# A broadcast read as 32 rows four times in place of 8 rows sixteen times, with a newly searched instruction order, in a two-layer linear-attention block

## Chip, cores and metric

The kernel runs on one core of one Trainium2 chip. The metric is the device time of one execution in microseconds (us), taken as the median of several executions. The program is straight-line code: 1618 operations before the change, put on the engines by a stored order that a search has found. One execution of each kernel was also recorded by the hardware profiler; all lines in profile fences below come from such records. "Span" is the time from the first to the last instruction in a record. It is about 1.7 us shorter than the device time of the same run.

## The reference, cut

```python
def _A_ref(x, wqkv, wo):                     # linear attention, 32 heads of 16
    q, k, v = split(x @ wqkv)                # (cut: reshape to heads)
    phi = lambda t: jnp.where(t > 0, t + 1, jnp.exp(t)) + 1e-6
    pq, pk = phi(q), phi(k)
    kv  = jnp.einsum("bhsd,bhse->bhde", pk, v)
    z   = jnp.einsum("bhsd->bhd", pk)
    num = jnp.einsum("bhqd,bhde->bhqe", pq, kv)
    den = jnp.einsum("bhqd,bhd->bhq", pq, z)[..., None] + 1e-6
    return merge_heads(num / den) @ wo
def _B_ref(x, w1, w2):                       # MLP, 512 -> 1376 -> 512
    return jnp.maximum(x @ w1, 0) @ w2
x = x + _A_ref(_layernorm(x), A_wqkv, A_wo)  # x: 1 x 2048 x 512, bfloat16
x = x + _B_ref(_layernorm(x), B_w1, B_w2)
x = x + _A_ref(_layernorm(x), A_wqkv, A_wo)
x = x + _B_ref(_layernorm(x), B_w1, B_w2)
```

The change concerns `den`. For each token and head there is one denominator, and all 16 elements of that head are divided by it. In the kernel the elements of eight heads lie on 128 partitions and 512 tokens lie along the free axis, so one row of reciprocals has to reach 16 partitions.

## The kernel before

The 2048 tokens are worked on in four chunks of 512, in each of the two attention layers, so the code below runs eight times. A small matmul against `Zc` writes the denominators of eight heads into 32 rows, each head four times. ScalarE forms the reciprocal as exp(-ln). Then the rows go out to DRAM and come back with every row repeated over 16 partitions, one DMA for each group of eight heads (`j`), and VectorE multiplies.

```python
def a_den_inv(t, b):
    us = [pq_unit(j, t) for j in range(4)]
    mm_group(lambda: [(psv[32*j:32*j+32, b, :], Zc[:, j, :], unit_ap(us[j]), True, True, False)
                      for j in range(4)], ...)
    ...                                                     # ACT: ln, then exp(-ln) -> rsp
    r = rdram[cur_layer[0] // 2, t]
    dma(lambda e: e.dma_start(r, rsp[:, s, :]), ...)        # L844, write
    for j in range(4):                                      # L847, broadcast
        i = 4 * t + j
        dma(lambda e, i=i, j=j: e.dma_start(xn[:, i, :],
            r[32*j:32*j+8, :].unsqueeze(1).broadcast_to([8, 16, 512])), [("rd", t)], [("xn", i)], 650.0, ...)

def a_den_mul(t, s, GB):                                    # L855, multiply
    for j in range(4):
        g.add(DVE, lambda e, j=j, i=i: e.tensor_tensor(unit_ap(us[j]), unit_ap(us[j]), xn[:, i, :], ALU.mult), ...)
```

Which head a row holds is decided by a mask made once on GpSimd. With the pattern `[[0, 4], [-16, 8]]` the eight heads come one after the other, and that four times over:

```python
e.affine_select(zm1[:],   onesf[:, 0:32], [[0, 4], [-16, 8]], ALU.is_ge, 0.0, base=0,  channel_multiplier=1)
e.affine_select(zmask[:], zm1[:],         [[0, 4], [16, 8]],  ALU.is_ge, 0.0, base=15, channel_multiplier=-1)
```

DMA transposes, issued on the same queue as the broadcasts, turn the normalised activations `xn` into `Tb`, which matmuls read:

```python
def tr_dma(lo, hi):                                         # L484
    dma(lambda e: e.dma_start_transpose(Tb[:, lo:hi, :, :]..., xn[:, lo:hi, :]...), ...)
```

Ten matmuls on zeros open the program on TensorE (`WARM`):

```python
for k in range(WARM):                                       # WARM = 10, on a tile of zeros
    last = e.matmul(psv[:, wt, :], wrm[:, 0:128], wrm[:, :], start=True, stop=True)
```

Two small constants, `ehead` and `esel`, are computed on VectorE by `den_consts()`; `esel` is made from `ehead`, and nothing reads `esel`. The order in which all operations are issued, and the memory bank of each matmul result, are two stored tables, `ORDER` and `BANKS`.

## Time and profile before

| | before |
|---|---|
| device time, 3 runs | 268.33, 268.69 and 552.36 us (median 268.69; the last counts as a slow run and is left out of every ratio) |
| span of the profiled run | 267.4 us (another run, of 269.12 us) |
| TensorE busy | 260.0 us, 97% |
| TensorE idle in the profiled run | 7.4 us: 2.0 in the first 10 us, 2.9 in the last 3.4 us, 2.5 between |
| broadcasts | 32 of 128 KB each, on 8 of 16 DMA engines |

How to read it: an engine that is 97% busy can be made faster only by the 7.4 us in which it stands, by gaps too short to show, or by less work. The change takes no work from TensorE. Two answers about single lines of the kernel before: count, then nanoseconds that the queue spends on issuing one (minimum, median, maximum), then the first and last start.

```profile
L844 SPq DMA_DIRECT2D rdram<-rsp x8: 322/334/572, 42.4 to 191.3; - x8
...
L847 SPq DMA_DIRECT2D xn<-rdram x32: 577/577/751, 44.2 to 197.6; - x32
```

The write and the broadcast move 128 KB each, but the broadcast takes the queue 577 ns and the write 334.

Last, the only wait of TensorE on a DMA, in the list of waits:

```profile
PE ps L538 <- DMA Tb<-xn: 1.0, 1, 1.0
```

It is one wait of 1.0 us, on a transpose.

### The profile page before, as it was taken

To read this page: it belongs to the slowest core of one execution; us is meant where nothing else is said; L and a number is where in the kernel's file an instruction comes from. 1 tells how busy PE (TensorE), PEld (TensorE's weight loads), DVE (VectorE), ACT (ScalarE), POOL (GpSimd) and SP (SyncE) were. 2 spreads that over 40 slices of the span, in tenths; PEclk is the share of its full clock that TensorE was granted. 3 is DMA by queue.
4 is the path that set the end of the run, shared out by engine and by line. 5 is a ranking of instruction groups with operands and counts; after the bars stand their busy time and mean duration, and the time that the engine had idled before them with its cause. 6 is when DMAs were issued, how large, how long until landed. Compare 5 with 4: busy or idle time off the path is not lost.

```text
span 267.4 us, 5269 instructions
## 1 busy us (share of the span) xinstructions
PE 260.0 (97%) x1919; PEld 171.5 (64%) x1937; DVE 240.7 (90%) x660; ACT 202.4 (76%) x446; POOL 19.6 (7%) x30
## 2 busy tenths in 40 slices
PE   7999999998999999999999999999999999999995
PEld 2444444546447888887875654454786778888883
DVE  4999999999789999999998998499989999889975
ACT  3999965889888786487788998799999869745320
POOL 4021000000030002201011000000000000130000
PEclk9999999999999999999999999999999999999999
DMA  6954882346234061401403400322592245201104
GB/s 209 382 115 82 195 306 71 127 78 162 38 107 91 0 81 21 82 0 22 77 13 69 78 2 2 103 93 43 131 175 50 39 42 99 81 0 22 80 2 157
DMA packets 47626, 23.61 MB, mean 88 GB/s; under 512 B 37008, under 2 KB 46192, under 8 KB 47600
## 3 DMA queue, kind: packets, MB, share of 16 engines
q1 hardware_dynamic: 47456, 23.24, 35.3%
q8 instruction: 15, 0.25, 0.4%
q14 instruction: 11, 0.09, 0.1%
q10 hardware_dynamic: 144, 0.03, 0.1%
HBM read 11.21 MB, written 3.15 MB: 54 GB/s over the span
## 4 chain that ended last, share of the span: by engine, by line
PE 85%; DVE 7%; DMA 5%; issue 1%; ACT 1%; SPq 0%; DVEq 0%
PE ps L538 84%; DMA Tb<-xn 3%; DMA xin<-in_A_x_dram 1%; DVE xres L551 1%; DVE xres L582 1%; DVE ps L1035 1%; DVE xn L970 1%; DVE xin L1061 1%; DVE xn L558 0%; ACT big L518 0%; PE ps L501 0%; DVE xn L578 0%; DVE bst L445 0%; DVE KVT L649 0%; ACT xn L556 0%
## 5 line engine op out<-in xcount | busy, mean ns | idle before, releaser
L520 ACT ACTIVATE escr<-ps 128x512 bf16<-128x512 f32 x56 | 33.3, 614 | 7.1 <-PE ps L538 7.0
L1021 ACT ACTIVATE big<-ps 128x512 bf16<-128x512 f32 (+1 forms) x57 | 29.2, 530 | 8.0 <-PE ps L538 7.7
L545 ACT ACTIVATE sqscr<-xres 128x512 bf16<-128x512 f32 x48 | 30.4, 633 | 5.3 <-DVE xres L582 2.6
L518 ACT ACTIVATE big<-ps 128x512 bf16<-128x512 f32 x56 | 33.3, 611 | 1.4 <-PE ps L538 1.3
L538 PE MATMUL ps<-big,xn 128*128 128x512 bf16 x122 | 30.2, 379 | 0.3
L538 PE MATMUL ps<-Tb,wqkv 128*128 128x512 bf16 x128 | 30.5, 379 | 0.0
L538 PE MATMUL ps<-gw,big 128*128 128x512 bf16 x121 | 29.2, 379 | 0.3
L538 PE MATMUL ps<-wqkv,Tb 128*128 128x512 bf16 x92 | 22.7, 379 | 0.7 <-ACT Tb L508 0.3
L524 DVE TENSOR_TENSOR big<-big,escr 128x512 bf16<-128x512 bf16 x56 | 22.4, 420 | 0.8 <-ACT big L518 0.2
L538 PE MATMUL ps<-w2s,big 128*128 128x256 f16 x160 | 21.9, 272 | 0.1
L538 PE MATMUL ps<-xn,w 128*128 128x256 f16 x140 | 21.8, 273 | 0.0
L538 PE MATMUL ps<-xn,xin 128*128 128x256 f16 x140 | 21.4, 273 | 0.2 <-DVE xn L970 0.2
L538 PE MATMUL ps<-w,big 128*128 128x256 f16 (+3 forms) x114 | 21.6, 301 | 0.0
L538 PEld LDWEIGHTS ps<-Tb,wqkv 128*128 128x128 bf16 x128 | 12.2, 98 | 14.3 <-issue 0.2
L538 PE MATMUL ps<-Tb,wper 128*128 128x256 bf16 x140 | 21.3, 272 | 0.0
L538 PEld LDWEIGHTS ps<-gw,big 128*128 128x128 bf16 x128 | 12.4, 98 | 12.7 <-issue 0.5
L538 PEld LDWEIGHTS ps<-big,xn 128*128 128x128 bf16 x128 | 12.0, 97 | 13.1 <-issue 0.7
L571 POOL TENSOR_TENSOR rstdf<-varf,nhalf 128x4 f32<-128x4 f32 x8 | 9.6, 1201 | 145.1 <-DVE varf L569 145.1
L538 PE MATMUL ps<-w,xin 128*128 128x256 bf16 (+2 forms) x145 | 19.7, 269 | 0.1
L1004 ACT ACTIVATE ps<-ps 128x512 f32<-128x512 f32 (+1 forms) x32 | 16.5, 514 | 4.4 <-PE ps L538 2.4
L1104 ACT ACTIVATE ps<-ps 128x256 f32<-128x256 f32 x27 | 10.0, 371 | 11.8 <-PE ps L538 10.3
L522 DVE TENSOR_SCALAR escr<-escr 128x512 bf16<-128x512 bf16 x56 | 15.6, 288 | 2.4 <-ACT escr L520 2.4
(160 smaller groups left out, 544.8 us busy)
## 6 DMA issues: line engine op xcount, KB each, us to landing
xn<-rdram SPq DMA_DIRECT2D x32, 128.0 KB
wqkv<-in_A_wqkv_dram SPq DMA_DIRECT2D x3, 512.0 KB, 7.1
xin<-in_A_x_dram SPq DMA_DIRECT2D x3, 512.0 KB, 7.9
out_dram<-xn SPq DMA_DIRECT2D x3, 512.0 KB, 2.6
w<-in_B_w_dram SPq DMA_DIRECT2D x1, 1376.0 KB, 6.9
w<-in_B_w_dram SPq DMA_DIRECT2D x1, 1280.0 KB, 9.9
rdram<-rsp SPq DMA_DIRECT2D x8, 128.0 KB, 1.7
wo<-in_A_wo_dram SPq DMA_DIRECT2D x1, 512.0 KB, 10.1
```

The costliest lines, as they stand in the source:

```text
L518: g.add(ACT, lambda e: e.activation(dst_ap, psv[:, b, :], ACTF.Identity, bias=1.0 + 1e-6, scale=1.0), [("ps", b)], [dst_key], C_ACT_PSUM, ...
L520: g.add(ACT, lambda e: e.activation(escr[:, s, :], psv[:, b, :], ACTF.Exp), [("ps", b)], [("escr", s)], C_ACT_EXP, name=name + "_exp")
L522: g.add(DVE, lambda e: e.tensor_scalar(escr[:, s, :], escr[:, s, :], 1.0, 1e-6, ALU.min, ALU.add), [("escr", s)], [("escr", s)], C_DVE_BF4 ...
L524: g.add(DVE, lambda e: e.tensor_tensor(dst_ap, dst_ap, escr[:, s, :], ALU.max), [dst_key, ("escr", s)], [dst_key], 340.0, name=name + "_phi")
L538: last = e.matmul(o, l, r, start=st, stop=sp, skip_group_check=skip)
L545: g.add(ACT, lambda e: e.activation(sqscr[:, q, :], xres[:, i, :], ACTF.Square, accum_out=dst[:, i:i + 1]), [("xres", i)], [("sqscr", q), ...
L551: g.add(DVE, lambda e: e.scalar_tensor_tensor(xres[:, i, :], psv[:, b, :], 0.0, src, ALU.add, ALU.add, accum_out=s1f[:, i:i + 1]), [("ps", ...
L571: g.add(POOL, lambda e: e.tensor_tensor(rstdf[:, sl], varf[:, sl], nhalf[:, 0:4], ALU.pow), [("varf", t), ("nhalf",)], [("rstdf", t)], C_P ...
L582: g.add(DVE, lambda e: e.scalar_tensor_tensor(xres[:, i, :], psv[:, b, :], rstdf[:, i:i + 1], xres[:, i, :], ALU.mult, ALU.add, accum_out= ...
L1004: g.add_flex([(ACT, lambda e: e.activation(dst(), psv[:, src, 0:W], ACTF.Identity), cost(C_ACT_PSUM)), (DVE, lambda e: e.tensor_copy(dst() ...
L1021: g.add_flex([(ACT, lambda e: e.activation(out_ap(r, m), pv(b), ACTF.Relu), cost(C_ACT_PSUM)), (DVE, lambda e: e.tensor_scalar(out_ap(r, m ...
L1104: g.add_flex([(ACT, lambda e: e.activation(psv[:, c1, cols], psv[:, c2, L], ACTF.Identity), 290.0), (DVE, lambda e: e.tensor_copy(psv[:, c ...
```

## The change

The intent is to bring the broadcast to all 16 DMA rings; a ring here is the part of the queue that one of the 16 DMA engines serves. The heads are laid out so that each head's four rows are neighbours. A group can then be read as 32 rows, each repeated four times, and 32 is a multiple of 16 where 8 is not. The two unused constants go. Then `ORDER` and `BANKS` are searched anew; in the new order 21 operations that may run on either VectorE or ScalarE changed sides, too.

```diff
-e.affine_select(zm1[:],   onesf[:, 0:32], [[0, 4], [-16, 8]], ...)
+e.affine_select(zm1[:],   onesf[:, 0:32], [[-16, 8], [0, 4]], ...)
-e.affine_select(zmask[:], zm1[:],         [[0, 4], [16, 8]],  ...)
+e.affine_select(zmask[:], zm1[:],         [[16, 8], [0, 4]],  ...)
...
-    e.dma_start(xn[:, i, :], r[32*j:32*j+8, :].unsqueeze(1).broadcast_to([8, 16, 512]))   # modelled at 650 ns
+    e.dma_start(xn[:, i, :], r[32*j:32*j+32, :].unsqueeze(1).broadcast_to([32, 4, 512]))  # modelled at 550 ns
...
-        def den_consts(): ...        # ehead: reduce_sum, esel: tensor_copy
-                        den_consts()
...
-ORDER = """ 17 0 14 12 15 18 13 ...   (1618 entries)
+ORDER = """ 17 0 14 12 15 18 13 ...   (1616 entries, other order; cut)
-BANKS = ("01346013225745647657647457...   (cut)
+BANKS = ("01346013225745647667664457...   (cut)
```

## The prediction

> **What bounds the kernel now.** I read the page first, then busy times by stretch, then the groups by line, then the chain that ended last, and last the two stretches in which the broadcasts run. The page's busy shares:
>
> ```profile
> PE 260.0 (97%) x1919; PEld 171.5 (64%) x1937; DVE 240.7 (90%) x660; ACT 202.4 (76%) x446; POOL 19.6 (7%) x30
> PE 85%; DVE 7%; DMA 5%; issue 1%; ACT 1%; SPq 0%; DVEq 0%
> ```
>
> The first line says TensorE is occupied in 260.0 of 267.4 us; the second, the chain of work that ended last by engine, says the same from behind: 85% of it is matmuls, and only 5% is DMA, which is the part that this change can touch. Busy time hides gaps shorter than a matmul's latency, so I rebuild TensorE's own time from the cadence. A run of 23 matmuls of 512 columns takes 5.13 us and one of them lasts 0.379, so the cadence is (5.13 - 0.379) / 22 = 0.216 us; four of 256 columns take 0.60 us with 0.273 for one, so (0.60 - 0.273) / 3 = 0.109 us. The program has 572 of the first (missing records filled in from the code) and about 1102 of the second: 123.5 + 120.6 us. With 128 of 96 columns at 0.042 (5.4), 60 of 128 columns at 0.056 (3.4), and some 3 us of tiny ones and denominators, TensorE needs about 255.9 us at full cadence. So **only 11.5 us of the 267.4 are not matmul cadence**. Where they are, by stretches (columns: stretch, its length, busy time of each engine):
>
> ```profile
> 0.00:10.00 10.00, 8.00 (x36) 3.06 (x37) 6.01 (x17) 5.03 (x14) 2.71 (x15) 1.00 0.80 270
> 51.00:70.00 19.00, 17.90 (x119) 9.59 (x119) 18.59 (x59) 16.41 (x35) 0.00 (x0) 1.00 0.50 102
> 186.00:206.00 20.00, 19.70 (x178) 15.03 (x178) 18.68 (x54) 19.43 (x48) 0.00 (x0) 1.00 0.60 125
> 264.00:267.40 3.40, 0.47 (x6) 0.29 (x6) 1.01 (x2) 0.00 (x0) 0.00 (x0) 1.00 0.32 96
> ```
>
> 2.0 us are the start, 2.9 the end (last evictions and stores); neither is touched by the diff. All the middle stretches together show 2.5 us of idle TensorE, of which 1.1 in 51 to 70 us and 0.3 in 186 to 206 us, and the remaining 4.1 us (11.5 - 2.0 - 2.9 - 2.5) are gaps too short to show. So everything that a better schedule could win is about 6.6 us, and I ask what part of that hangs on the broadcasts.
>
> The waits and the timeline around those two stretches answer that:
>
> ```profile
> 59.41 0.34 SPq L844 DMA_DIRECT2D rdram<-rsp  x1
> 60.27 2.64 SPq L484 DMA_TRANSPOSE Tb<-xn  x2
> 62.95 2.49 SPq L847 DMA_DIRECT2D xn<-rdram  x4
> 65.48 1.21 SPq L881 DMA_TRANSPOSE big<-hrt  x1
> ...
> 66.65 1.69 PE L538 MATMUL ps<-Tb,w 128*128 128x512 bf16 x7 [1.05 <-DMA Tb<-xn]
> ...
> 198.83 0.42 DVE L970 TENSOR_TENSOR xn<-xn,Tb 128x512 f16<-128x512 f16 x1 [0.90 <-DMA Tb<-xn]
> ```
>
> The reader sees that no engine is shown waiting for the broadcast itself (L847); what TensorE and VectorE wait for is a DMA transpose that shares the queue with it. The transpose issued at 61.6 us landed after 5.0 us, the one at 194.4, in between eight broadcasts, after 4.4 us; most transposes of this trace land after 3.0 to 3.2.
>
> That the broadcast uses half of the DMA engines is visible while eight of them run with nothing beside them (last two columns: mean share of the 16 DMA engines, GB/s):
>
> ```profile
> 46.00:48.00 2.00, 2.00 (x23) 1.38 (x21) 1.59 (x5) 1.91 (x4) 0.00 (x0) 1.00 0.51 175
> 48.00:50.00 2.00, 2.00 (x11) 0.80 (x9) 1.85 (x5) 1.45 (x4) 0.00 (x0) 1.00 0.52 184
> ```
>
> A share of 0.51 is eight engines full and eight empty.
>
> **What the Trainium skill says.** (1) "DMA: Bandwidth & Descriptors", section "Why a DMA increments its semaphore by 16 and not by 1": the number of engines k is the largest one up to 16 that divides the slowest non-trivial dimension of both access patterns. An 8-row source against 128 partitions gives 8, a 32-row source gives 16. The 0.51 agrees for the kernel before. (2) Same page, "Specifications": about 27 GiB/s for one engine. The trace gives 180 GB/s over eight, 22.5 GB/s each, so the measured number is used. (3) Same page, "Queues, rings and completion order": on each engine descriptors are consumed in ring order, so a transpose issued behind four broadcasts waits for them. The 4.4 us landing at 194.4 fits that; the 5.0 us one was issued ahead of its broadcasts, so ring order alone does not explain it. (4) "Perfetto Trace Analysis", section "Identifying the Most-Contended Engine": matmul occupancy is no measure of distance to the limit; hence the cadence sum above.
>
> **The change part by part.**
>
> *Broadcast transfers.* 32 DMAs of 128 KB, in eight chunks of four. At 180 GB/s one takes 131072 / 180000 = 0.73 us of its eight rings; four take 2.9 us, longer than their issue (4 x 0.62 = 2.49 us). On 16 rings at 22.5 GB/s each, one is an estimated 0.36 us. The data then wait for the issue. The issue itself is 0.577 us now; the plain 16-ring write of the same 128 KB (L844) issues in 0.33 us and 16-ring loads with a three-dimensional pattern in about 0.43, so I estimate 0.43, a spacing of about 0.48, and 4 x 0.48 = 1.9 us for a chunk. The last broadcast of a chunk of four lands about 2.9 - (3 x 0.48 + 0.36) = 1.1 us earlier. For the pair of chunks at 44 to 51 us it is about 5.8 - (7 x 0.48 + 0.36) = 2.1 us.
>
> *What of it is on the path.* The multiplies that read the broadcasts (L855, 32 times 418 ns) show 0.0 us of idle VectorE ahead of them: the tuned order already places them behind the landing. So an earlier landing is worth nothing at the old places; it pays where the transposes share the rings, and where the new order can put multiplies earlier. First place: TensorE's 1.05 us at 66.6, from a transpose 1.8 us late. If the lateness halves with the ring time of the broadcasts, 0.9 us returns. Second place: the transpose at 194.4 would be issued about 4 x 0.14 = 0.6 us earlier and find rings with half the work; VectorE waited 0.9 us there, but TensorE stood only 0.20 visibly, so I count 0.3. Elsewhere 0.2 for short gaps. Together 1.4 us if all is kept.
>
> *Two constants removed.* 0.20 us (L823) and 0.22 us (L825) on VectorE at 40.6 and 43.8 us. TensorE is 1.95 of 2.00 us busy there, so most is hidden: 0.1 us.
>
> *Mask order and denominators.* The two mask operations on GpSimd have the same shapes, and so has the denominator matmul (four of 128x32 by 512, 0.40 us a group). Only the order of the rows changes: 0.
>
> *A newly searched order and bank table.* The diff's longest part. It removes no work, moves everything by a few tenths, and was searched on a model of times. The middle stretches have 6.6 us of loss whatever the order, and it may shift either way; I take a spread of about 1 us around zero, and expect that half of the 1.4 us is kept: the waits of a dense schedule are replaced by the next ones. Sum: 268.69 - 0.7 - 0.1 = 267.9 us.
>
> **The rivals.** (a) *The transfer is hidden anyway.* Nothing waits for L847 by name, VectorE is 90% busy and TensorE 97%; then only the reordering remains and the time is 268.5 +- 0.7. For it speaks the 0.0 ahead of L855; against it the two late transposes. (b) *A new collision takes the place of the old one.* The broadcasts now occupy all 16 engines and not half of them, so that transposes and stores find no free engine; and an order searched on modelled durations packs them closer. Then a transpose lands as late as before in another place and TensorE stands 1 to 2 us: 269.5 to 270.5. For it speaks that the late transposes sit next to broadcasts; against it that the total ring time of a broadcast does not grow, so that the slowest ring gets less. (c) *The schedule really gets looser.* If both waits vanish and the short gaps shrink by a third as well, 1.4 + 1.4 = 2.8 us: 265.9. Against it: the 255.9 us of cadence and the ends are untouched, and these gaps are mostly VectorE's and ScalarE's latencies.
>
> **Range and chances.** The centre is 267.9. Rival (b) sets the upper end, cut as its worse half needs an order worse than the old one, which its author would hardly have kept: 269.5. Rival (c) sets the lower end at 266.1. Faster by over 2% would need 5.4 us of the 6.6 us that any order could win: 0.01. Slower by over 2% needs an unlucky collision of 5 us: 0.02.
>
> **What would show it.** Right: while broadcasts run alone the DMA share is well above 0.52 or the traffic comes in shorter bursts; L847 issues in clearly less than 577 ns; the wait of TensorE for a transpose near 66 us is under 0.6 us; the group L855 still shows no idle ahead; the two lines of constants are gone; TensorE's busy count per shape is unchanged. Wrong: L847 still at 577 ns, or transposes landing at 4.4 us or more beside the broadcasts in more places than now. What would make the time wrong is the new order: middle idle of TensorE over 4 us (slower), or a start shorter than 2.0 us, which I take as fixed.

## More of the kernel before

Next, the stretch after the first pair of broadcast chunks (stretch, length, busy time of TensorE, its weight loads, VectorE, ScalarE and GpSimd, granted clock, share of the 16 DMA engines, GB/s):

```profile
50.00:52.00 2.00, 1.95 (x10) 0.88 (x9) 2.00 (x8) 2.00 (x5) 0.00 (x0) 1.00 0.39 137
```

The last broadcast was issued before 49.3 us, yet DMA engines are still busy in this stretch: transfer lags behind issue.

## The result

The changed kernel takes 267.06 us (median of 4 runs, 266.58 to 267.14) against 268.69 us for the kernel before (median of its three fast runs, 268.33 to 269.00; with the slow run of 552.36 counted in, the median is 268.85). The ratio is 0.9936, with a 95% interval of 0.9915 to 0.9958. A ratio is the mean time of one kernel's fast runs over that of the other's in the same rounds, so it is not quite the ratio of the medians quoted beside it. A later repetition (x6 below) gave 0.9923 (0.9906 to 0.9940). It is a real gain of about 0.7%. The span of the profiled run went from 267.4 to 265.3 us. The result is correct.

The page of the changed kernel, busy times and the chain that ended last:

```profile
PE 259.3 (98%) x1919; PEld 172.3 (65%) x1937; DVE 241.4 (91%) x661; ACT 201.1 (76%) x443; POOL 18.7 (7%) x30
...
PE 91%; DVE 4%; ACT 2%; DMA 1%; issue 1%; SPq 0%; DVEq 0%
```

The instruction count of TensorE is the same. DMA has gone from 5% of the chain to 1%. The same stretches as before, in the changed kernel:

```profile
0.00:10.00 10.00, 7.89 (x37) 3.14 (x38) 5.98 (x17) 5.11 (x14) 2.80 (x15) 1.00 0.80 266
46.00:48.00 2.00, 2.00 (x23) 1.39 (x22) 1.59 (x5) 2.00 (x4) 0.00 (x0) 1.00 0.61 201
48.00:50.00 2.00, 2.00 (x10) 0.79 (x9) 2.00 (x6) 1.45 (x4) 0.00 (x0) 1.00 0.62 196
50.00:52.00 2.00, 1.95 (x10) 0.90 (x10) 1.93 (x7) 2.00 (x5) 0.00 (x0) 1.00 0.21 66
51.00:70.00 19.00, 18.95 (x129) 10.78 (x128) 18.57 (x60) 17.52 (x40) 0.00 (x0) 1.00 0.44 98
186.00:206.00 20.00, 19.95 (x186) 15.88 (x185) 18.95 (x53) 19.43 (x50) 0.55 (x1) 1.00 0.50 111
262.00:265.30 3.30, 0.42 (x6) 0.24 (x5) 0.95 (x2) 0.00 (x0) 0.00 (x0) 0.89 0.33 99
```

Read from these and those of before, TensorE's idle time fell from 7.4 to 6.0 us: 0.1 more at the start, the same 2.9 at the end, and between them 1.0 in place of 2.5. The stretch from 51 to 70 us gave 1.05 of that (busy 17.90 to 18.95) and the one from 186 to 206 us gave 0.25. The other 0.7 us of the span is less occupied time (260.0 to 259.3) for the same matmuls: gaps too short to be counted as idle. The DMA share while broadcasts run alone rose from 0.51 to 0.61, at 201 in place of 175 GB/s. It did not double.

Why it did not is in the queue's timeline from the first broadcasts to the first of the two places (start, length of the group, engine, line):

```profile
44.08 5.12 SPq L837 DMA_DIRECT2D xn<-rdram  x8
...
58.68 0.34 SPq L834 DMA_DIRECT2D rdram<-rsp  x1
59.91 2.65 SPq L482 DMA_TRANSPOSE Tb<-xn  x2
62.60 3.29 SPq L837 DMA_DIRECT2D xn<-rdram  x4
65.94 1.28 SPq L871 DMA_TRANSPOSE big<-hrt  x1
```

and in the broadcast's own line, with the answer's line on its landing times:

```profile
L837 SPq DMA_DIRECT2D xn<-rdram x32: 519/603/1362, 44.1 to 196.0; - x32
...
DMA to landing us min/median/max: 2.2/2.5/4.0
```

Before, the same places were:

```profile
44.16 5.10 SPq L847 DMA_DIRECT2D xn<-rdram  x8
...
62.95 2.49 SPq L847 DMA_DIRECT2D xn<-rdram  x4
```

Eight broadcasts are issued in 5.12 us, one every 0.64, as before (5.10). The median issue is 603 ns, a little longer than the 577 of the 8-ring form. 131,072 bytes every 0.64 us are 205 GB/s, which is what the windows show: on 16 rings the queue's issue, no longer the rings, seems to set the pace (x3 tests this). Beside the transposes the chunk of four even takes longer than before, 3.29 us in place of 2.49, as one of its issues stands for 1.36 us; e2, on 16 rings in the old order, shows the same (3.42), and e1, on 8 rings in the new order, does not (2.48).

The wait of TensorE at 66.6 us is gone. These are the same matmuls in TensorE's timeline after, with no wait ahead of them:

```profile
65.33 1.89 PE L536 MATMUL ps<-Tb,w 128*128 128x512 bf16 x8
```

The transpose ahead of it landed after 3.1 us in place of 5.0, and the later one, issued at 193.3 us, after 3.5 in place of 4.4. The multiplies show what they showed before, 32 times 415 ns with 0.0 us of idle ahead.

### The profile page after: what moved, and what is told of

Read it like the earlier page. It is cut to its first block, busy times and chain, and to the rows that moved or that the text cites. A ratio compares the mean times of both kernels' runs of the same rounds, so it can differ in the third digit from the quotient of the medians.

```text
span 265.3 us, 5276 instructions
## 1 busy us (share of the span) xinstructions
PE 259.3 (98%) x1919; PEld 172.3 (65%) x1937; DVE 241.4 (91%) x661; ACT 201.1 (76%) x443; POOL 18.7 (7%) x30
## 4 chain that ended last, share of the span: by engine, by line
PE 91%; DVE 4%; ACT 2%; DMA 1%; issue 1%; SPq 0%; DVEq 0%
PE ps L536 91%; DVE bst L443 2%; DMA xin<-in_A_x_dram 1%; ACT big L1011 1%; DVE big L522 0%; ACT lden L994 0%; DVE escr L520 0%; DVE xn L475 0%; ACT ps L994 0%; DVE xn L576 0%; PE ps L499 0%; DVE KVT L647 0%; DVE xn L1165 0%; ACT sqscr L543 0%; ACT Tb L506 0%
## 5 line engine op out<-in xcount | busy, mean ns | idle before, releaser
L518 ACT ACTIVATE escr<-ps 128x512 bf16<-128x512 f32 x56 | 32.7, 612 | 7.7 <-PE ps L536 7.5
L516 ACT ACTIVATE big<-ps 128x512 bf16<-128x512 f32 x56 | 32.6, 612 | 1.4 <-PE ps L536 1.3
L522 DVE TENSOR_TENSOR big<-big,escr 128x512 bf16<-128x512 bf16 x56 | 22.5, 420 | 1.0 <-ACT big L516 0.2
L536 PE MATMUL ps<-xn,xin 128*128 128x256 f16 x140 | 22.0, 272 | 0.0
L536 PE MATMUL ps<-w,big 128*128 128x256 f16 (+2 forms) x114 | 21.6, 301 | 0.0
L569 POOL TENSOR_TENSOR rstdf<-varf,nhalf 128x4 f32<-128x4 f32 x8 | 8.5, 1065 | 147.2 <-DVE varf L567 147.2
```

Source lines behind the costliest of these rows:

```text
L516: g.add(ACT, lambda e: e.activation(dst_ap, psv[:, b, :], ACTF.Identity, bias=1.0 + 1e-6, scale=1.0), [("ps", b)], [dst_key], C_ACT_PSUM, ...
L518: g.add(ACT, lambda e: e.activation(escr[:, s, :], psv[:, b, :], ACTF.Exp), [("ps", b)], [("escr", s)], C_ACT_EXP, name=name + "_exp")
L522: g.add(DVE, lambda e: e.tensor_tensor(dst_ap, dst_ap, escr[:, s, :], ALU.max), [dst_key, ("escr", s)], [dst_key], 340.0, name=name + "_phi")
L536: last = e.matmul(o, l, r, start=st, stop=sp, skip_group_check=skip)
L569: g.add(POOL, lambda e: e.tensor_tensor(rstdf[:, sl], varf[:, sl], nhalf[:, 0:4], ALU.pow), [("varf", t), ("nhalf",)], [("rstdf", t)], C_P ...
```

## The experiments

The result left three questions. Which part of the change brings the gain: the rings, the order, or the removed constants? Why did the transpose before 66.6 us land late? And is the broadcast's issue the new limit? My theory (the prediction's) was that the 8-ring broadcasts held the transposes up. One rival was that the new order alone does it. A second rival came up, and the later experiments test it.

That second rival is the instruction fetch. The page of both kernels counts a queue named "instruction" (q8) with 15 packets of 16 KB. Here are the DMA queues in the 2 us in which the late transpose of the kernel before was finishing (packets, MB, share of 16 engines):

```profile
q1 hardware_dynamic: 412, 0.29, 47.7%
q8 instruction: 1, 0.02, 2.9%
```

A transpose runs on all 16 rings, and each ring reports by itself: its semaphore is updated sixteen times in every run. I worked the reports out of the semaphore events of the trace. For the transpose that TensorE waits for at 66.6 us, fifteen of the sixteen rings reported between 64.82 and 65.06 us and one at 66.60. The instruction packet started at 64.51 and took 0.92 us. The same computation for this place in every run:

```
run                               fetch packet starts   the sixteen rings report (us)
before                            64.51                 15: 64.82 - 65.06    one: 66.60
e3 old order,  8 rings            64.01                 15: 64.38 - 64.50    one: 66.00
e2 old order, 16 rings            64.75                 16: 66.77 - 66.88
e4 old order, 16 rings            64.01                 16: 66.22 - 66.33
x8 old order, 16 rings, shifted   64.41                 15: 64.71 - 64.88    one: 66.42
x1 before, fetch moved            57.6                  16: 64.66 - 64.80
x5 old order, 16 rings, moved     58.3                  16: 65.29 - 65.41
after                             63.71                 16: 64.23 - 64.40
e1 new order,  8 rings            64.29                 16: 64.57 - 64.81
x6 after, again                   63.33                 16: 63.73 - 63.89
x3 after, plain read              63.30                 16: 63.91 - 64.04
x4 one broadcast                  66.33                 16: 65.45 - 65.64
x2 after, shifted                 63.66                 15: 64.02 - 64.14    one: 65.71
x7 after, fetch moved             58.0                  16: 64.48 - 64.60
```

The place is not the only one. The 14 records hold 420 transposes from `xn` to `Tb`. In 32 of them a packet of q8 starts 0.7 to 2.3 us after the issue; all 32 landed late, after 3.74 to 5.46 us. In 308 no packet starts from 1.5 us before the issue to 3.05 us after; 285 of those landed within 3.4 us. A packet 2.3 to 3.05 us after the issue, near the end of the transpose as here, goes either way: 22 landed after 4.49 us or more, 16 within 3.3. In the kernel before, the transposes issued at 95.8, 140.1 and 213.7 us also landed late (4.26, 4.80 and 3.98 us), each with a packet and with no broadcast near. A second queue of this kind (q14, packets of 8 KB) is no rival: near this place it has a packet in runs with and without a late ring (65.15 before, 65.48 in x1), and at 140.1 us a ring is late with none near.

The Trainium skill, "Runtime: NRT & Kernel Launch", section "Instruction fetch mechanics", states that each engine's sequencer refills its instruction memory in 16 KiB blocks of 256 instructions through a DMA queue, at a cost that is mostly hidden. The trace agrees on the size. Fifteen blocks of 256 are 3840 instructions, and the page counts 1919 + 1937 = 3856 matmuls and weight loads, so I take these packets for TensorE's. That gave a means to move a packet: put extra instructions on TensorE at the start, in the warm-up on zeros. They don't hold up what follows: the first matmul after the warm-up starts at 5.54 to 6.09 us with 60 of them (x1, x5, x7) and at 5.43 to 6.34 in the runs without.

### e1: the new order on 8 rings

The edit undoes masks and source in the changed kernel and keeps its order:

```diff
-[[-16, 8], [0, 4]] / [[16, 8], [0, 4]],  r[32*j:32*j+32, :].unsqueeze(1).broadcast_to([32, 4, 512])
+[[0, 4], [-16, 8]] / [[0, 4], [16, 8]],  r[32*j:32*j+8,  :].unsqueeze(1).broadcast_to([8, 16, 512])
```

> The changed kernel with its order and without the two constants, but the old mask order and the 8-row broadcast (8 rings). If the gain of 1.8 us comes from the wider broadcast, this loses most of it: ratio to before above 0.997, and a transpose near 61 us lands late again (4 us or more). Rival, the gain is the newly searched order: ratio stays at 0.993 to 0.995. A third possibility, the new order relies on earlier landings: VectorE waits for broadcasts by name and the ratio goes above 1.000.

Measured: 267.95 us against 268.46, ratio 0.9970 (0.9951 to 0.9990). The wait near 66 us is gone here, too, though the broadcasts run on 8 rings: with the new order alone the transpose lands in 3.3 us. A wait at the second place is there instead, in TensorE's timeline:

```profile
198.33 0.61 PE L536 MATMUL ps<-Tb,wper 128*128 128x256 bf16 x4 [0.79 <-DMA Tb<-xn]
```

and in the busy times of that stretch:

```profile
186.00:206.00 20.00, 19.21 (x178) 15.10 (x177) 18.20 (x50) 18.93 (x47) 0.00 (x0) 1.00 0.56 115
```

TensorE is busy for 19.21 us there, against 19.95 on 16 rings in the same order. Neither forecast fits whole: the ratio lies at the edge of the first, the landing is the one of the second. So the order brings about 0.3%, and the 16 rings remove this wait, in another place than I had put most of the gain. That they add the rest of the gain follows from the ratios less firmly: the interval of e1 overlaps that of 0.9936 and not that of 0.9923, and all three come from different sets of runs. VectorE also waits here for broadcasts, three times, 0.8 us in all, off TensorE's path.

### e2: the old order on 16 rings

The edit is the masks and the source of the diff in the kernel before, and nothing else.

> The kernel before with only the two masks and the broadcast changed (16 rings), order and constants as before. If the wider broadcast brings the gain itself, the transpose issued at 61.6 us lands in about 3.1 us and not 5.0, TensorE's wait of 1.05 us at 66.6 us is gone and the ratio is 0.994 to 0.997. If the order brings it, the ratio is 0.998 to 1.002 and the transpose is late as before.

Measured: 268.74 us against 268.46, ratio 0.9997 (0.9979 to 1.0016). The rings alone bring nothing that shows, with the fetch still in place. TensorE's wait is the one of before:

```profile
PE ps L538 <- DMA Tb<-xn: 1.0, 1, 1.0
```

This is against the prediction's reason for the first place: there the ring time of the broadcasts was to be the cause, and halving it left 1.0 us of wait standing. The second place did behave as reckoned:

```profile
186.00:206.00 20.00, 20.00 (x183) 15.52 (x181) 19.20 (x54) 19.79 (x49) 0.00 (x0) 1.00 0.61 128
```

TensorE is fully busy there (19.70 before), and still the time is the same.

### e3 and e4: the constants taken out as well

The edit removes `den_consts`, its call and its two entries of the order, from the kernel before (e3) and from e2 (e4).

> The kernel before with only the two constants removed (0.42 us of VectorE). Both theories: hidden, ratio 0.999 to 1.001. A ratio below 0.998 would mean that VectorE is the bound near 41 us after all.

> All of the change but the new order and bank table: 16 rings, no constants, old order. Ring theory: 0.994 to 0.997, as the run with the rings alone. Order theory: 0.998 to 1.001; the difference to the changed kernel (0.9936) is then what the order brings.

Measured: e3 269.27 us, ratio 1.0029 (1.0007 to 1.0051); e4 268.36 us, ratio 0.9988 (0.9971 to 1.0005), against the same 268.46. There is no gain from the constants: e3 is even a little slower than the kernel before, above what was expected. Its trace shows three waits of TensorE of 0.5 us each that are shorter or absent before; why the shift brings them isn't known. e4 is within the noise of e2. In e4 the wait of TensorE near 66 us is 0.9 us. Each of e2, e3 and e4, like the kernel before, had a fetch packet at the tail of that transpose and at least one late ring, as the table shows.

### x1: the kernel before, with the fetch moved away

The edit adds 30 matmuls and 30 weight loads on zeros at the start; the columns in all stay the same (40 x 128 in place of 10 x 512):

```diff
-WARM=10;  e.matmul(psv[:, wt, :],     wrm[:, 0:128], wrm[:, :],     ...)
+WARM=40;  e.matmul(psv[:, wt, 0:128], wrm[:, 0:128], wrm[:, 0:128], ...)
```

> The kernel before, with its 10 warm-up matmuls of 512 columns cut into 40 of 128: the same columns, but 60 more TensorE instructions ahead of everything, so that each 16 KB fetch of TensorE's instructions comes some 4 to 6 us earlier against the rest. Theory (the late transpose near 61.6 us is one ring held up by such a fetch): the fetch that was at 64.5 us comes near 60, that transpose lands in 3.1 to 3.3 us on all sixteen rings, the wait of 1.05 us at 66.6 us is gone, and the ratio to before is 0.995 to 0.997. Rival (broadcasts on half the rings make it late): it still lands after 4.6 us or more and the ratio is 0.999 to 1.001.

Measured: 268.73 us against 269.04, ratio 0.9977 (0.9954 to 1.0001). The fetch moved to 57.6 us, all sixteen rings of the transpose reported within 0.14 us, and the wait at 66.6 us vanished, with the broadcasts still on 8 rings. So the fetch was the cause of that wait. But little of the microsecond remained at the end (the ratio is above the forecast of 0.995 to 0.997, and its interval reaches 1), for a loss came up at the second place:

```profile
PE ps L538 <- DVE xn L970: 1.3, 1, 1.3
```

```profile
186.00:206.00 20.00, 18.66 (x175) 14.67 (x174) 17.70 (x49) 18.33 (x46) 0.00 (x0) 1.00 0.63 116
```

The first fence is the list of TensorE's waits, the second the stretch. TensorE waits 1.3 us for VectorE's token sums (L970), which themselves waited 2.0 us for the transpose among the 8-ring broadcasts. But the shift had brought a fetch packet here, too. It starts at 195.02 us and takes 1.79 us, and the transpose, issued at 192.96, lands after 5.46 us in place of 4.37 in the kernel before. The DMA queues from 194 to 196 us and the line of that transpose show it:

```profile
q8 instruction: 1, 0.02, 5.6%
...
DMA to landing us min/median/max: 5.5/5.5/5.5
```

So x1 does not tell what the 8 rings alone cost at the second place; e1 does.

### x2: the changed kernel, with the fetch moved back

The edit is a warm-up of 16 matmuls of 320 columns, six more pairs of instructions:

```diff
-WARM=10;  e.matmul(psv[:, wt, :],     wrm[:, 0:128], wrm[:, :],     ...)
+WARM=16;  e.matmul(psv[:, wt, 0:320], wrm[:, 0:128], wrm[:, 0:320], ...)
```

> The changed kernel, with the warm-up cut into 16 matmuls of 320 columns: 12 more TensorE instructions, so that the fetch seen at 63.7 us, just after the transpose issued at 61.3 us had left its ring, comes some 0.4 us earlier, into that transpose. Theory: one ring (or all) of that transpose lands 1 us or more late, TensorE waits 0.3 to 1 us for it near 66 us, ratio 0.995 to 0.998 against the 0.9936 of the changed kernel. Rival: the landing stays at 3.1 us and the ratio at 0.993 to 0.994.

Measured: 267.99 us against 269.04, ratio 0.9954 (0.9933 to 0.9974). One ring reports late again (65.71, the others by 64.14), and TensorE's wait is back in the changed kernel:

```profile
PE ps L536 <- DMA Tb<-xn: 0.7, 1, 0.7
```

Nothing but the number and width of the matmuls on zeros was changed. So the wait was switched off in the kernel before (x1) and on in the changed one (x2). The shift itself did not go as forecast: the packet was to come 0.4 us earlier, and against the issue of the transpose it came later (2.81 us after it, 2.41 in the changed kernel and 2.52 in its repetition x6). That it then met the transpose was luck; why a few instructions move it this way isn't known. The median is 0.9 us above that of the changed kernel in the first measurement, but in another set of runs, and the intervals of the two ratios overlap; the wait, not the total, is what this run shows.

### x3: the same bytes without the repetition

The edit reads the 128 rows once, in place of 32 rows four times. The result is wrong (relative error 0.17); the bytes and the rings are the same.

```diff
-e.dma_start(xn[:, i, :], r[32*j:32*j+32, :].unsqueeze(1).broadcast_to([32, 4, 512]))
+e.dma_start(xn[:, i, :], r)
```

> The changed kernel with each broadcast read replaced by a plain read of the same 128 KB, 128 different rows on 128 partitions (wrong result on purpose: the quotients use wrong denominators). It asks what the issue of a broadcast costs: if the repeated-row pattern is what makes the issue 0.60 us, it falls to about 0.33 us, a chunk of four is issued in 1.5 us and not 2.5, and the ratio is 0.990 to 0.993, as the prediction took for granted in part. If it stays near 0.60 us, the issue depends on something else, and the ratio stays at 0.993 to 0.995.

Measured: 266.8 us against 269.04, ratio 0.9912 (0.9885 to 0.9938). The issue fell:

```profile
L837 SPq DMA_DIRECT2D xn<-rdram x32: 319/432/1571, 43.7 to 194.7; - x32
```

The median is 432 ns in place of 603 (0.33 us had been expected), and a chunk of four with no transposes beside it is issued in 1.74 us. So 0.17 us of the issue belong to the repeated, three-dimensional source pattern. The stretch of the broadcasts shows that the issue had set the pace; with the same bytes and rings, 0.61 and 201 GB/s have become

```profile
46.00:48.00 2.00, 2.00 (x22) 1.28 (x20) 1.59 (x5) 1.65 (x4) 0.00 (x0) 1.00 0.92 285
```

The time is not told apart from that of the changed kernel (0.9936 and 0.9923; the intervals overlap). The ratios differ by 0.3 to 0.6 us, which the noise does not tell from nothing.

### x4: one broadcast in place of four

The edit writes the reciprocals interleaved, so that one DMA of 512 KB on 16 rings brings all four groups:

```diff
-dma_start(r, rsp[:, s, :])
+dma_start(r.rearrange("(q j) d -> j q d", j=4), rsp[:, s, :])
-for j in range(4): dma_start(xn[:, 4*t+j, :], r[32*j:32*j+32, :].unsqueeze(1).broadcast_to([32, 4, 512]))
+dma_start(xn[:, 4*t:4*t+4, :]..., r.rearrange("(q j) d -> q (j d)", j=4).unsqueeze(1).broadcast_to([32, 4, 2048]))
```

> The changed kernel with one broadcast of 512 KB a chunk in place of four of 128 KB (32 rows of 4 KB, four times), which needs the denominators written with rows interleaved, a write whose outermost dimension is 4. The issue of a chunk shrinks from 2.5 us to about 0.6, but the write runs on 4 rings: 131 KB at 4 x 22 GB/s takes 1.5 us and not 0.4, and nothing of a chunk is usable before all of it landed. If the queue's issue time is what limits, ratio 0.990 to 0.993; if the latency of the first multiply counts, 0.995 to 1.002.

Measured: 276.37 us against 269.04, ratio 1.0280 (1.0239 to 1.0321), a correct result and clearly slower, which no forecast had. The broadcasts land after 3.8 us (2.5 for the small ones), all four groups together, and the multiply that could start after the first group now stands. The edit slows the write, too: in the undisturbed chunk at 75 us the interleaved write (on 4 rings: its semaphore is updated 5 times, that of an 8-ring broadcast 9 times) landed after 3.26 us in place of 1.69 for the plain one at 72.5 us of the changed kernel, and the broadcast is issued only then. The two lines are from the list of waits:

```profile
PE ps L535 <- DVE big L843: 4.3, 2, 2.8
...
DVE big L843 <- DMA xn<-rdram: 5.7, 5, 1.9
```

So two things cost time here, a later first quarter (about 1.3 us) and a later write (about 1.6 us), and the run doesn't tell their shares apart. The order was not searched anew for the large DMA, so the run says nothing against it in another order.

### x5, x6 and x7: rings and fetch apart from the order

x5 is e2 with the 60 more instructions of x1, so that the old order on 16 rings would meet no fetch. x6 is the changed kernel again. x7 is the changed kernel with the same 60 instructions. All three ran on one chip.

> Old order, 16 rings (as the second run of the first set, ratio 0.9997), with TensorE's instruction fetches moved by 60 instructions. Theory: two losses of about 1 us each stand one behind the other in the kernel before. The one at 66 us comes from the fetch on one ring, and the one at 194 to 199 us from a transpose behind broadcasts on 8 rings; whoever removes only one shifts most of it to the other. With both removed in the old order: no wait of TensorE for a transpose near 66 us nor near 198 us, ratio 0.992 to 0.995, with no new order at all. Rival (the searched order is better in itself): the ratio stays at 0.997 to 1.000.

> The changed kernel as it is, beside the others on one chip: 0.992 to 0.995 by all theories. The reference for the runs of this set.

> The changed kernel with the fetches moved by 60 instructions, which may beat both kernels: the two transposes that still had one late ring (at 141 us, no wait of TensorE behind it) get their fetch elsewhere. TensorE shows only about 1 us of idle time between 10 and 262 us, so theory: at most 0.5 us better than the changed kernel, ratio 0.991 to 0.994; or, where a moved fetch meets another transpose with TensorE behind it, up to 1 us worse, 0.995 to 0.998.

Measured, against 268.74: x5 268.16 us, ratio 0.9972 (0.9952 to 0.9992); x6 266.75 us, 0.9923 (0.9906 to 0.9940); x7 268.04 us, 0.9969 (0.9949 to 0.9990).

x5 missed its expectation of 0.992 to 0.995. The wait near 66 us was gone, but the shift had brought another fetch packet to 195.1 us, onto the second transpose. That one landed after 4.85 us (3.46 in e2), and TensorE stood 0.7 us there for VectorE's sums that read it. The same happened to the changed kernel in x7, within its second forecast, where the transpose issued at 193.4 us met a packet at 195.3 and landed after 4.84 us:

```profile
PE ps L536 <- DMA Tb<-xn: 0.9, 1, 0.9
```

```profile
186.00:206.00 20.00, 19.08 (x177) 14.99 (x176) 18.02 (x49) 18.86 (x47) 0.00 (x0) 1.00 0.53 112
```

x6 against x7 is the cleanest pair: same chip, same order, same rings, same work apart from zeros at the start. Their intervals do not overlap, and they differ by 1.3 us in the median, 0.9 of which is the one wait for a transpose that met a fetch packet.

### x8: the old order on 16 rings, with the fetch moved later

The edit is `WARM=8` in e2, to move the packets later by four instructions.

> Old order and 16 rings (ratio 0.9997 before), with two of the ten warm-up matmuls left out: 4 TensorE instructions fewer, so that the fetch that came 2.7 us after the issue of the transpose near 62 us comes about 0.4 us later, behind it, and the fetch near 201 us stays clear of the transpose near 195. Theory (both losses are collisions on the DMA rings): that transpose lands in 3.1 to 3.3 us, no wait of TensorE near 66 us, none above 0.3 us near 198, ratio 0.993 to 0.996 without a new order. Rival (the new order is better in itself): 0.998 to 1.000. If the fetch still hits the transpose the run says nothing and shows 0.999 to 1.001.

Measured: 268.55 us against 269.01, ratio 1.0001 (0.9974 to 1.0029). The four instructions did not move the packet against the transpose (2.75 us after its issue; 2.76 in e2), and it still met it (one ring at 66.42, the others by 64.88; TensorE waits 0.8 us). This leaves the question as it was. An old order on 16 rings that meets no fetch at either place was not reached, so how much the rings alone would bring there stays open.

## Why the prediction was right, and where its steps were not

The predicted 267.9 us was 0.8 us above the measured 267.06, within the range of 266.1 to 269.5, and "within 2%" was the outcome given 0.97. The gain was forecast at 0.8 us and measured at 1.6. The steps held to different degrees, and the number owes part of its fit to luck.

**The frame held.** The 255.9 us of cadence (1102 times 0.109 is 120.1 and not 120.6, so 255.4 by its own figures) and the two ends were taken as out of reach, and they were: the end lost 2.9 us before and after, the start 2.0 and 2.1. All that was won came from the middle, 1.5 us of visible idle time and 0.7 us of short gaps, out of the 6.6 us that the prediction had left open. This is why the gain could not come near 2%.

**The 16 rings held, the shorter issue did not.** The DMA share rose above 0.52, as the row rule of the cited page had it. The estimate of 0.43 us for the issue was wrong: it is 0.603, and the spacing 0.64 and not 0.48. The prediction had named this as a sign of being wrong ("L847 still at 577 ns"), and it came. The step that failed is the one that took the figure from 16-ring loads with a three-dimensional pattern. x3 shows that the repeated source costs the difference. The pair of chunks was to land 2.1 us earlier. With the spacing as measured, the same formula gives 5.8 - (7 x 0.64 + 0.36) = 1.0 us. The semaphore events agree: the last of the eight landed 7.9 us after the first was issued before (52.05) and 7.0 after (51.11). None of this reached the time through the multiplies, which had no wait to lose.

**The first place: the size was right, the cause was wrong.** The prediction gave 0.9 us back at 66.6 us "if the lateness halves with the ring time of the broadcasts". The 1.05 us did come back, by luck as far as this reason goes. For e2 and e4 show that 16 rings leave the wait standing in the old order (1.0 and 0.9 us), e1 shows that it goes on 8 rings in the new order, and x1 and x2 switch it off and on by moving a 16 KB instruction packet. In the new order the packet starts 2.41 us after the issue of the transpose in place of 2.88, and no ring is late. In e1 it starts 2.75 us after, and none is late either, though x8 has a late ring at 2.75; what decides there isn't known. The prediction itself had noted that ring order did not explain this transpose, since it was issued ahead of its broadcasts; I should have taken that as a reason to look for other traffic, and listed the DMA queues of that stretch. Its remark that the late transposes sit next to broadcasts did not hold for the kernel before: those at 95.8, 140.1 and 213.7 us had none near.

**The second place: the mechanism was right, the term too small.** The transpose among the broadcasts was to gain from less ring work, and 0.3 us was counted because TensorE stood only 0.20 us there. Where no fetch packet came before its landing, it landed after 4.4, 4.6 and 4.7 us on 8 rings (before, e1, e3) and after 3.2 to 3.6 on 16 (after, e2, e4, x2, x3, x6, x8). With the new order on 8 rings (e1) TensorE waits 0.79 us at this place, and on 16 rings 0.0. From e1 to the changed kernel the ratio falls by 0.34 to 0.47 points (0.9970 to 0.9936 and 0.9923), which is 0.9 to 1.3 us, across different sets of runs. The term was read from how the old order happened to stand there; that the first wait had already made TensorE late is my reading, and no run shows it apart from the order.

**The two do not add up.** The rings alone bring nothing that shows (0.9997), the new order alone 0.3% (0.9970), both together 0.64% to 0.77% (0.9936, 0.9923). My explanation is that a wait late in the program is hidden by one ahead of it, so that the time falls only where both are gone. It fits e1 and e2, but the run that would show it, the old order on 16 rings with no fetch at either place, was not reached. The prediction's advice to count half of 1.4 us, as the next wait takes the place of each, fits the new order alone; it was too high for the rings alone and too low for both together.

**The new order was not "a spread of about 1 us around zero".** It brought some 0.5 to 0.8 us by itself (e1). There TensorE's idle time fell from 1.10 to 0.20 us in the stretch of the first place and rose from 0.30 to 0.79 in that of the second, so the first wait is more than the whole of it. That is luck as much as search: the model of times in the kernel's code, on which the order is searched, has no entry for the fetch, and 60 instructions on zeros (x7) take 1.3 us back.

**The constants.** Counted at 0.1 us, they brought nothing (1.0029 and 0.9988).

**The rivals.** (a), that the transfer is hidden anyway, is true of the multiplies and of the rings alone. (b), a new collision with the broadcasts on all 16 engines, did not come; the late transposes of x2, x5 and x7 met a fetch packet. (c), 265.9 us, was too bold by 1.2 us, though its idea, that short gaps would shrink as well, gave 0.7 us.

**What stays open.** The packet takes 0.9 us and the late ring reports 1.5 us after the others. The Trainium skill, "DMA: Bandwidth & Descriptors", section "Queues, rings and completion order", states that a ring's increment of the semaphore lands only after every earlier write of that engine, across its queues. That would fit a report held up by the fetch's write, but no run here shows it. Nor do the traces show on which ring a packet runs. In the kernel before and in e1 the transpose's last data packet ended within 0.01 us of the fetch's start; in the one a ring was late, in the other none. In e2 and e4 the last data packets of the transpose itself, 5 and 20 of them, started only after the fetch had ended, 19 and 18 packets of broadcasts took 1.1 to 1.6 us each, and all sixteen rings reported late. Why that takes another form than one late ring isn't known.

## What to carry to other kernels

When a DMA lands late, list every queue that moved bytes in that stretch, the instruction queue too, before blaming the neighbour that you can see in the source: here a few instructions on zeros at the start moved the wait or made it go. Widening a DMA from 8 to 16 rings helps only until its issue sets the pace, so look up the issue time of the very pattern that you will use. And test the parts of a change singly and together: two waits in a row can hide each other, and each part alone may seem worth nothing. Shifting a fetch also shifts the ones behind it: look at every transpose again (x1, x5, x7).

## What the Trainium skill lacked or had wrong

- "Runtime: NRT & Kernel Launch", "Instruction fetch mechanics", calls the cost of crossing a 16 KiB block mostly hidden. For TensorE's own instructions nothing here speaks against it, but the page does not say that such a packet can hold up a data transfer. ("DMA: Bandwidth & Descriptors" lists a row for refill among the queues that each DMA engine serves in turn, but gives no cost.) The transpose before 66 us reported 1.5 us late on one ring (64.82 to 65.06 us against 66.60) or on all sixteen (66.77 to 66.88), and cost TensorE 0.7 to 1.05 us; 32 of 32 transposes with a packet 0.7 to 2.3 us after their issue landed after 3.74 to 5.46 us. There are 15 such packets in the run, of 0.88 to 1.45 us in the kernel before.
- "DMA: Bandwidth & Descriptors", "Issuing engines are not separate DMA queues", calls the time to initiate a DMA usually small relative to the DMA. Here it is not: a broadcast of 128 KB holds its queue for 0.603 us, and the queue's pace (0.64 us each, 205 GB/s) is the limit on 16 rings; with an issue of 0.432 us the same stretch moves 285 GB/s (x3).
- The same page gives no issue time by access pattern. Measured for 128 KB: 0.33 us for a plain write, a median of 0.43 for a plain read, 0.577 for 8 rows repeated 16 times, 0.603 for 32 rows repeated 4 times.
- The same page, "Specifications", gives about 27 GiB/s for one engine. Eight full engines moved 180 GB/s here, 22.5 each, with packets of 1 KB.
- No page tells what a ring held up does to a transpose that runs on all sixteen: here anything between one late report and a standstill of about 1 us, in which 18 or 19 other packets took 1.1 to 1.6 us.
